# Two more blocks of an MLP by seven products of quarters, two fewer as filler for attention

## The chip, the cores and the metric

One core of a Trainium2 chip. The metric is the device time of one execution in microseconds (us); each kernel was run several times, and a profile was taken of one execution. On one core a run's state can only be told by its distance from the fastest run of the same kernel; every run used here counts as fast. Engines: PE is TensorE, PEld its weight loads, DVE VectorE, ACT ScalarE, POOL GpSimd, SP SyncE; a "q" behind a name is the engine's queue of issues and waits.

## The reference, cut to what matters

```python
# 8 batches x 8 heads, 576 rows of 64; then an MLP of 4608 tokens, 512 -> 2048 -> 512, all float32
scores = scale * q @ k.T
scores = np.where(scores >= scores.max(-1) - tau, scores, -1e9)
attn = np.exp(scores - scores.max(-1)); attn = attn / (attn.sum(-1) + 1e-9)
x = heads_side_by_side(attn @ v)            # 4608 x 512
h = x @ w_in                                # 4608 x 2048
out = (0.5 * h * (1 + erf(h / sqrt(2)))) @ w_out
```

## The kernel before

Attention goes by pairs of heads, 32 in all, each in five chunks: four of 128 rows for both heads, one with the last 64 rows of both. The MLP goes by 18 blocks of 256 tokens. Ten of them are "plain": they are dealt out between the chunks as filler, so that TensorE has work while DVE does the softmax. The last eight are done at the end in four "duos", each two blocks by seven products of quarters in place of eight (a matrix product cut into quarters takes eight smaller products, or seven and some more sums).

What matters for this study is how a pair's results come together. After the softmax of a chunk DVE transposes it in 32 by 32 squares; SyncE then issues copies that regroup the squares, for chunks 0 and 1 together, 2 and 3 together, and the short chunk. The row sums become divisors, which this kernel sends through DRAM to spread them over the partitions; in the next pair's chunk 2, P is multiplied by V, and DVE divides the product.

```python
def divisors(p):                                   # after chunk 4
    ...                                            # DVE: add, reciprocal, transpose the sums
    nc.sync.dma_start(rows..., turned)             # L401: sums to DRAM
    for e in range(2):
        nc.sync.dma_start(to[:, 0:MAIN]..., src)   # L407: divisors back, to every partition
        nc.sync.dma_start(to[:, MAIN:S]..., src)   # L409

def regroup(p, i):
    for a in range(4):
        if i == NC:                                # the short chunk: 4 "tail" copies, L432
            nc.sync.dma_start(s["pT"][e][...], pd_tail[p % 2][rows])
            continue
        for e in (1, 0):                           # 8 copies after chunk 2, 8 after chunk 3, L436
            nc.sync.dma_start(s["pT"][e][...][:, :, half], pd[e][rows, :, half])

# one chunk of pair p (cut; made[] are the two divisions of the pair before, in chunk 2 only)
scores(p, i); softmax_head(p, i)                   # PE; DVE reduce, ACT exp, DVE threshold
softmax_tail(p, i)                                 # DVE multiply by the mask, with the row sum
if made: made[0]()                                 # DVE L466, waits for the divisors
turn_p(p, i)                                       # DVE transposes
if made: made[1]()
if i == 2: regroup(p, 1)
if i > 2: regroup(p, i)
if i == NC: divisors(p)
if i == 1: load(p + 2)                             # 16 loads of q, k, v issued by GpSimd
if i == 2: turn_qk(p + 1)                          # DVE transposes of the next pair's q and k
fill(...)                                          # PE: filler from the plain blocks
```

## Time and profile before

| | before |
|---|---|
| median of its first 3 runs | 1435.5 us (1433.5 to 1439.47) |
| span of the profiled run | 1434.2 us |
| pair period in the attention, pairs 4 to 31 | (1008.6 - 179.9) / 27 = 30.7 us |
| busy TensorE in that stretch | 99% |
| four duos, 1037.3 to the end | 397 us |

The lines that carry the prediction stand in it. Three more of the same view of waits are needed for the comparison: engine and line, what it waited for, us in total, times, longest.

```profile
DVE p L379 <- ACT p L361: 25.0, 51, 1.1
...
DVE x L466 <- PE xT L448: 7.9, 3, 3.2
...
PE sc L349 <- DVE p L379: 8.5, 11, 2.9
```

The first is DVE at its masked multiply, waiting for ScalarE's exp; the second DVE at its division, waiting for the product to divide; the last is TensorE at the scores, waiting for DVE to free the banks. All are small beside DVE's own wait for TensorE's scores, 105.5 us in the prediction: mostly it is TensorE that is late.

### The profile page before, as it was taken

What the parts mean: (1) busy time and instruction counts of PE and PEld (TensorE: products, weight loads), DVE (VectorE), ACT (ScalarE), POOL (GpSimd) and SP (SyncE); (2) the same over time, 40 slices, a digit from 0 to 9 for tenths busy, and PEclk for the clock granted to TensorE, in tenths of its full rate; (3) what the DMA queues carried; (4) which work ended last, traced back from release to release, by engine and by line L of the source; (5) the groups of instructions that cost most, each with busy time, mean ns of one, the idle gap of its engine ahead of it and who ended that gap; (6) DMA issues with size and microseconds to landing.
All of it is one profiled execution on the core that took longest, in us unless ns stands there. A gap on an engine that the chain in (4) does not pass through costs nothing.

```text
span 1434.2 us, 19357 instructions
## 1 busy us (share of the span) xinstructions
PE 1389.7 (97%) x6544; PEld 962.9 (67%) x6544; DVE 941.1 (66%) x2088; ACT 640.3 (45%) x1039; POOL 288.0 (20%) x502
## 2 busy tenths in 40 slices
PE   6899899999999999999999999999999999999999
PEld 5667546566466574664756647566488888888887
DVE  5987887886777878778788778777664132241330
ACT  5758525436355264472654726547142141230320
POOL 3121323422222433223332224300000000000000
PEclk8999999999999999999999999999999999999999
DMA  9967368897777898778988788875500100100000
GB/s 281 275 243 202 113 133 151 140 161 130 125 137 122 151 150 151 145 125 142 168 146 155 154 142 152 142 143 106 107 1 1 44 1 0 59 0 8 23 1 30
DMA packets 449489, 167.04 MB, mean 116 GB/s; under 512 B 413040, under 2 KB 432048, under 8 KB 449392
## 3 DMA queue, kind: packets, MB, share of 16 engines
q1 hardware_dynamic: 423184, 108.65, 43.0%
q0 software_dynamic: 23808, 56.57, 14.8%
q8 instruction: 53, 0.87, 0.3%
q10 hardware_dynamic: 2400, 0.59, 0.2%
q14 instruction: 44, 0.36, 0.1%
HBM read 71.68 MB, written 11.47 MB: 58 GB/s over the span
## 4 chain that ended last, share of the span: by engine, by line
PE 85%; DVE 8%; ACT 3%; DMA 1%; issue 1%; SPq 0%; DVEq 0%; ACTq 0%
PE bank L629 27%; PE hT L508 18%; PE o_ps L520 17%; PE sc L349 12%; PE xT L448 10%; DVE p L379 2%; DVE nmx L360 2%; ACT p L361 1%; DVE power L185 1%; PE tr L295 1%; DMA inv<-turned 1%; DVE mant L183 0%; DVE w_in L187 0%; ACT L488 0%; ACT L495 0%
## 5 line engine op out<-in xcount | busy, mean ns | idle before, releaser
L361 ACT ACTIVATE p<-sc,nmx 128x576 f32<-128x576 f32 x288 | 202.8, 740 | 405.2 <-DVE nmx L360 404.9
L508 PE MATMUL hT<-x,w_in 128*128 128x256 f32 x1280 | 297.3, 384 | 1.8 <-DVE x L466 1.7
L520 PE MATMUL o_ps<-w_out,g 128*128 128x512 f32 x640 | 294.6, 603 | 0.0
L508 PEld LDWEIGHTS hT<-x,w_in 128*128 128x128 f32 x1280 | 238.9, 190 | 60.0 <-issue 28.4
L360 DVE TENSOR_REDUCE nmx<-sc 128x1 f32<-128x576 f32 x288 | 205.0, 749 | 106.1 <-PE sc L349 105.5
L379 DVE SCALAR_TENSOR_TENSOR p<-sc,thr,p 128x576 f32<-128x576 f32 x288 | 225.3, 816 | 36.4 <-ACT p L361 25.0
L520 PEld LDWEIGHTS o_ps<-w_out,g 128*128 128x128 f32 x640 | 116.9, 190 | 140.7 <-issue 138.9
L448 PE MATMUL xT<-pT,v 128*64 128x288 f32 (+2 forms) x1280 | 169.4, 418 | 6.0 <-issue 5.4
L349 PE MATMUL sc<-kT,qT 64*128 64x288 f32 x960 | 167.0, 435 | 5.6 <-DVE p L379 5.2
L421 DVE STREAM_TRANSPOSE pd<-p 128x576 f32<-128x576 f32 x224 | 160.7, 756 | 3.0
L219 POOL DMA_DIRECT2D q<-in_q_dram x104 | 69.6, 675 | 462.7 <-DVE q_tail L337 349.7
L349 PEld LDWEIGHTS sc<-kT,qT 64*128 64x128 f32 x960 | 94.0, 188 | 87.7 <-issue 74.0
L448 PEld LDWEIGHTS xT<-pT,v 128*64 128x64 f32 x1280 | 93.6, 140 | 77.9 <-issue 22.7
L227 POOL DMA_DIRECT2D v<-in_v_dram x208 | 109.3, 528 | 58.6 <-DMA k<-in_k_dram 32.0
L629 PE MATMUL bank<-x,w_in 128*128 128x256 f32 x384 | 93.6, 379 | 3.2 <-DVE x L643 3.2
L495 ACT ACT_TABLE_LOAD x71 | 91.1, 1283 | 1.3
L488 ACT ACT_TABLE_LOAD x71 | 91.1, 1283 | 1.3
L629 PE MATMUL bank<-unit 128*128 128x256 f32 x352 | 87.7, 379 | 0.0
L629 PEld LDWEIGHTS bank<-x,w_in 128*128 128x128 f32 x384 | 72.9, 190 | 13.9 <-issue 4.1
L629 PEld LDWEIGHTS bank<-unit 128*128 128x128 f32 x352 | 66.9, 190 | 9.1
L629 PE MATMUL bank<-w_out,unit 128*128 128x256 f32 x320 | 72.3, 379 | 0.0
L219 POOL DMA_DIRECT2D k<-in_k_dram x104 | 68.7, 667 | 0.0
(143 smaller groups left out, 1279.9 us busy)
## 6 DMA issues: line engine op xcount, KB each, us to landing
pT<-pd SPq DMA_DIRECT2D x448, 160.0 KB, 4.8
pT<-pd_tail SPq DMA_DIRECT2D x112, 80.0 KB, 2.7
q<-in_q_dram POOLq DMA_DIRECT2D x104, 72.0 KB, 4.5
k<-in_k_dram POOLq DMA_DIRECT2D x104, 72.0 KB, 5.8
out_dram<-o_sb SPq DMA_DIRECT2D x28, 256.0 KB, 3.7
inv<-turned SPq DMA_DIRECT2D x56, 128.0 KB, 3.6
v<-in_v_dram POOLq DMA_DIRECT2D x156, 40.0 KB, 5.3
raw<-in_moe_w_out_dram POOLq DMA_DIRECT2D x10, 512.0 KB, 5.0
```

The costliest lines, as they stand in the source:

```text
L219: eng.dma_start(t[e * D + f:e * D + f + Q], rows[:, :, f:f + Q])
L227: eng.dma_start(t[r:P:4, e, 0:n, :], rows[:, r * KR:r * KR + n, :])
L349: nc.tensor.matmul(sc[e][:, h, 0:HALF], lhsT=lhsT, rhs=s["kT"][rows, at:at + HALF], start=True, stop=True)
L360: nc.vector.tensor_reduce(nmx[:, e:e + 1], sc, axis=AXIS.XY, op=ALU.max, negate=True)
L361: nc.scalar.activation(w[:, e * S:(e + 1) * S].rearrange("p (h s) -> p h s", h=2), sc, AF.Exp, bias=nmx[:, e:e + 1], scale=1.0)
L379: nc.vector.scalar_tensor_tensor(row, sc[e][:, :, 0:HALF], thr[:, e:e + 1], row, op0=ALU.is_ge, op1=ALU.mult, accum_out=den[e])
L421: nc.vector.transpose(to[:, 0:NB, :], w[:, e * S:(e + 1) * S].rearrange("p (b i) -> p b i", i=Q))
L448: nc.tensor.matmul(xT[f, 0:hi - lo], lhsT=s["v"][:, e, c, :], rhs=pT[:, c, lo:hi], start=(c == 0), stop=(c == KR - 1))
L488: nc.scalar.activation(t, hT, AF.Gelu)
L508: nc.tensor.matmul(hT[:, j % 2, :], lhsT=w_in_sb[c][:, j * P:(j + 1) * P], rhs=x_blk[n][:, c, :], start=(c == 0), stop=(c == N_DM - 1))
L520: nc.tensor.matmul(o[:, 0:d_model], lhsT=g[j][:, m * P:(m + 1) * P], rhs=w_out_sb[j], start=(j == 0), stop=(j == N_DF - 1))
L629: nc.tensor.matmul(to, lhsT=l, rhs=r, start=start and k == 0, stop=k == len(pairs) - 1, skip_group_check=not start)
```

## The change

Its intent: seven products are cheaper than eight, so do ten blocks that way; the attention then has less filler and should get shorter, and DVE and the loads are relieved so that it can.

```diff
-    PLAIN = N_BLK - 8
-    AWAY = [PLAIN, PLAIN + 1, PLAIN + 2]
+    PLAIN = N_BLK - 10
+    AWAY = list(range(PLAIN, PLAIN + 5))          # inputs of these blocks wait in DRAM
...
 def softmax_head(p, i):
     for e in range(n):
         nc.vector.tensor_reduce(nmx[:, e:e + 1], sc, ...)
+        nc.gpsimd.tensor_scalar(thr[:, e:e + 1], nmx[:, e:e + 1], -1.0, tau_eff, ...)
         nc.scalar.activation(w..., sc, AF.Exp, bias=nmx[:, e:e + 1], scale=1.0)
-    nc.vector.tensor_scalar(thr[:, 0:n], nmx[:, 0:n], -1.0, tau_eff, ...)
...
         if p >= HP and i == 1 and p + 2 < NP:
-            load(p + 2)
+            loads = load_steps(p + 2)
+        if p >= HP:
+            next(loads, None)                     # q, k, v, v: four issues a chunk
...
-    GOAL += [... [1.96, 3.3, 4.64, 5.98, 7.32, 8.66, PLAIN]]
+    GOAL += [... [1.75, 2.79, 3.83, 4.87, 5.92, 6.96, PLAIN]]
```

Cut from it: in the first four pairs the addition to the row sum goes to GpSimd and the reciprocal comes after the weight conversions; the conversions are paced a little faster, end with the first batch, and use another buffer for their last pieces.

More of the change, by code (lines that the diff above doesn't have):

```diff
@@ L67 @@
     N_BLK = B * S // TOK
-    PLAIN = N_BLK - 8
-    AWAY = [PLAIN, PLAIN + 1, PLAIN + 2]
-    order = list(range(PLAIN + 3, N_BLK)) + AWAY
+    PLAIN = N_BLK - 10
+    AWAY = list(range(PLAIN, PLAIN + 5))
+    order = list(range(PLAIN + 5, N_BLK)) + AWAY
     DUOS = list(zip(order[0::2], order[1::2]))
@@ L147, in load_piece @@
         k = loaded[0] - 1
-        if k % 2 and k < len(pieces) - 4:
+        if k % 2:
             room = pd[k // 2 % 2][:, 0:NB - 2, :].bitcast(U32).rearrange("p b i -> p (b i)")
@@ L210, in load, with load_steps @@
     def load(p):
+        for _ in load_steps(p):
+            pass
+    def load_steps(p):
         b, hp = divmod(p, HP)
@@ L219, in load @@
                     eng.dma_start(t[e * D + f:e * D + f + Q], rows[:, :, f:f + Q])
+            yield
         t = s["v"] = v_sb[p % 4]
@@ L227, in load @@
                 eng.dma_start(t[r:P:4, e, 0:n, :], rows[:, r * KR:r * KR + n, :])
+            yield
     def load_early(p):
@@ L356, in softmax_head @@
         nmx = small.tile([P, 2], FP32, tag="nmx", name="nmx")
+        thr = s["thr", i] = small.tile([P, 2], FP32, tag="thr", name="thr")
         w = s["p", i] = work.tile([P, 2 * S], FP32, tag="p", name="p")
@@ L360, in softmax_head @@
             nc.vector.tensor_reduce(nmx[:, e:e + 1], sc, axis=AXIS.XY, op=ALU.max, negate=True)
+            nc.gpsimd.tensor_scalar(
+                thr[:, e:e + 1], nmx[:, e:e + 1], -1.0, tau_eff, op0=ALU.mult, op1=ALU.subtract)
             nc.scalar.activation(
                 w[:, e * S:(e + 1) * S].rearrange("p (h s) -> p h s", h=2), sc, AF.Exp, bias=nmx[:, e:e + 1], scale=1.0)
-        thr = s["thr", i] = small.tile([P, 2], FP32, tag="thr", name="thr")
-        nc.vector.tensor_scalar(thr[:, 0:n], nmx[:, 0:n], -1.0, tau_eff, op0=ALU.mult, op1=ALU.subtract)
     def softmax_tail(p, i):
@@ L380, in softmax_tail, with diagonal @@
                 row, sc[e][:, :, 0:HALF], thr[:, e:e + 1], row, op0=ALU.is_ge, op1=ALU.mult, accum_out=den[e])
-        if p >= EARLY:
-            return
-        rden = small.tile([P, 2], FP32, tag="rden", name="rden")
-        nc.vector.tensor_scalar(pair[:, 0:n], pair[:, 0:n], 1e-9, None, op0=ALU.add)
-        nc.vector.reciprocal(rden[:, 0:n], pair[:, 0:n])
+        if p < EARLY:
+            nc.gpsimd.tensor_scalar(pair[:, 0:n], pair[:, 0:n], 1e-9, None, op0=ALU.add)
+            s["sum", i] = pair[:, 0:n]
+    def diagonal(p, i):
+        s = st[p]
+        den = s.pop(("sum", i))
+        n = den.shape[1]
+        nc.vector.reciprocal(den, den)
         diag = s["diag", i] = dg.tile([P, 2, P], FP32, tag="inv", name="diag")
         for e in range(n):
-            nc.scalar.activation(diag[:, e, :], ident, AF.Copy, bias=0.0, scale=rden[:, e:e + 1])
+            nc.scalar.activation(diag[:, e, :], ident, AF.Copy, bias=0.0, scale=den[:, e:e + 1])
     def divisors(p):
@@ L757 @@
     GOAL = [(-1, 0.0), (START - 1, 0.0), (BATCH - 1, 0.55)]
-    GOAL += [(BATCH * (m + 2) + WEIGH, x) for m, x in enumerate([1.96, 3.3, 4.64, 5.98, 7.32, 8.66, PLAIN])]
+    GOAL += [(BATCH * (m + 2) + WEIGH, x) for m, x in enumerate([1.75, 2.79, 3.83, 4.87, 5.92, 6.96, PLAIN])]
     def goal(n):
@@ L771 @@
     due = []
+    loads = iter(())
     for n in range(len(slots) + WEIGH + 1):
@@ L827 @@
         if p >= HP and i == 1 and p + 2 < NP:
-            load(p + 2)
+            loads = load_steps(p + 2)
+        if p >= HP:
+            next(loads, None)
         if p >= HP - 1 and i == 2 and p + 1 < NP:
             turn_qk(p + 1)
-        convert(3000 if n < 2 * HP else 3400)
+        convert(3000 if n < 2 * HP else 3650 if n < BATCH - 1 else 1e9)
+        if early:
+            diagonal(p, i)
         if not early:
```

## The prediction

> **What bounds the kernel now.** I read the page first, then stretches of the span, then the chain of waits, then single instructions in order of time around one attention pair, with the SyncE queue beside them.
>
> ```profile
> PE 1389.7 (97%) x6544; PEld 962.9 (67%) x6544; DVE 941.1 (66%) x2088; ACT 640.3 (45%) x1039; POOL 288.0 (20%) x502
> ...
> 180.00:1008.60 828.60, 819.26 (x3781) 499.30 (x3779) 654.56 (x1412) 415.33 (x551) 238.03 (x401) 1.00 0.81 142
> 1037.30:1434.00 396.70, 388.20 (x1793) 339.81 (x1791) 125.69 (x300) 102.06 (x258) 0.00 (x0) 1.00 0.04 16
> ```
>
> Columns of the last two: stretch, length, busy PE, PEld, DVE, ACT, POOL, granted clock, DMA share, GB/s. The first stretch is the attention of pairs 4 to 31, with ten plain MLP blocks as filler for TensorE; the second is the four duos (two blocks each) by seven products. TensorE is busy for 99% of the first, so the plain reading is "take filler out and the stage shrinks by as much". But DVE is at 79% and DMA at 0.81 there, so I looked for what comes next.
>
> ```profile
> 613.96 20.39 SPq L436 DMA_DIRECT2D pT<-pd  x16
> 634.45 3.37 SPq L432 DMA_DIRECT2D pT<-pd_tail  x4
> 637.92 0.58 SPq L401 DMA_DIRECT2D turned<-turned  x1
> 639.94 0.59 SPq L407 DMA_DIRECT2D inv<-turned  x1
> ...
> 644.39 17.92 SPq L436 DMA_DIRECT2D pT<-pd  x16
> ```
>
> One pair takes 644.39 - 613.96 = 30.4 us, and SyncE is issuing for some 27 of them. The pair's transfers hang together: 16 regroup copies (L436), 4 tails, the row sums to DRAM, four loads of divisors. DVE waits for the last of these:
>
> ```profile
> 553.29 0.52 DVE L466 TENSOR_TENSOR x<-xT,inv 128x64 f32<-128x64 f32 x2 [0.96 <-DMA inv<-turned]
> 553.73 1.43 DVE L421 STREAM_TRANSPOSE pd<-p 128x576 f32<-128x576 f32 x2
> ...
> DVE nmx L360 <- PE sc L349: 105.5, 101, 7.0
> ...
> DVE x L466 <- DMA inv<-turned: 34.7, 19, 5.2
> ...
> SPq L436 <- DVE pd L421: 74.9, 25, 44.7
> ```
>
> This is a ring. Divisors land, DVE divides, transposes chunk 2, turns the next q and k, does chunk 3 (reduce, threshold, multiply, transpose); then SyncE issues the second eight L436, the tails, the sums and the divisors, which land. Read instruction by instruction over all 27 rounds: landing to the start of the second eight is 8.0 to 10 us mostly, median 9.0; from there to the next landing 19.7 to 22.5, median 20.9, but 18.3 to 19.2 in the last rounds, which have no loads of q, k and v. Sum 29.9 against a period of 30.7 on average (27 periods from 179.9 to 1008.6). So TensorE and this ring are nearly balanced now; the ring has about 1 us of slack.
>
> **What the Trainium skill says.** "Perfetto Trace Analysis", What "DMA-bound" means: one of its forms is an issuing engine's track solid with DMA slices. SyncE at some 27 of 30.4 us agrees. "DMA: Bandwidth & Descriptors", Issuing engines are not separate DMA queues: all run on the same 16 DMA engines and interleave. Here too: with the loads absent (948 to 1009 us) the DMA share falls from 0.81 to 0.60 and the ring's SyncE half by 2 us. "GPSIMD Engine Reference", 4.1 Engine selection, prefers VectorE for elementwise work; for one element per partition this should not matter, but the trace has no such GpSimd operation (nearest: its 128x1 memset, 93 ns). "SBUF — State Buffer", SBUF: two separate sides: GpSimd and VectorE can lock each other out of a shared port pair; nothing in this trace shows it.
>
> **The change part by part.**
> 1. Two plain blocks leave the attention. A block has 128 instructions of 256 columns (20 take 4.32 us in the duos, 0.216 each: 27.6) and 64 of 512 (10 take 4.32 to 4.49: 28.2), so 55.3 to 56; two are -111 us of TensorE.
> 2. A fifth duo comes in. The chain of waits gives the others back to back, 1088.86, 1186.33, 1283.81, 1381.28: 97.5 us each. TensorE is its limit (DVE 126 of 397), and all of it is on the path: +97.5. TensorE alone would net -13, that is 0.9%.
> 3. Filler for a pair falls from 1.34/4 to 1.04/4 of a block: 4.15 us less, so TensorE needs 30.4 - 4.15 = 26.3 us for a pair.
> 4. The threshold leaves DVE: 138 x 238 ns = 32.8 us over 28 pairs, with gaps some 0.33 us a chunk. DVE was 654.6/27.1 = 24.1 us a pair, now 23.0; with the exp it waits for in the short fifth chunk and small waits for scores about 25.3. In the ring only chunk 3's threshold lies: 9.0 - 0.35, and a further 0.7 because TensorE no longer comes late with scores; I take 7.8 (shortest seen with the threshold 8.0 to 8.2). On GpSimd it lies beside the exp (740 ns), so it costs nothing unless GpSimd is issuing.
> 5. The loads: 16 issues at 0.53 to 0.68 us, 9.6 us a pair, now four at a time (2.1 to 2.7 us) behind a chunk's thresholds. The next threshold is due some 4.6 us later, so it fits. q and k go out with chunks 1 and 2, and leave the second eight's window: L436 there 9.8 us, 7.3 without loads, now about 8.2. But they then meet the sums and divisors, which I let grow by about 1. Half ring 20.9 - 1.6 + 1 = 20.2.
> 6. Two more blocks to DRAM and back: four transfers of 512 KB at 5 us, hidden; about 1 us of SyncE each.
> 7. First 180 us: thresholds, additions and part of the division's waiting leave DVE (20 x 0.4 us), conversions end earlier; DVE is over 90% busy in much of it, so about -6.
>
> Ring: 7.8 + 20.2 = 28.0 us for a pair, above TensorE's 26.3 and DVE's 25.3; the last pairs without loads nearer 26.5, so 27.7 on average. Sum: start 179.9 - 6 = 174; 27 x 27.7 = 748; rest of the last pair 26 (was 28.7); duos 396.9 + 97.5 = 494.4. Together 1442. I put 1441.
>
> **The rivals.**
> A, TensorE stays the limit: 27 x 26.5 = 716, total about 1410. For it: 99% busy now, DVE kept down on purpose, and a tuned kernel's next step is likely to have been kept for a gain. Against: the ring's 29.9, of which the change shortens only parts.
> B, as worked out: the ring of divisors, DVE and SyncE is the new bound; about four fifths of the stage's gain of 111 goes, 1441. For it: DVE waits for the divisors in most rounds already.
> C, DMA fills up: the same descriptors in less time. 0.81 x 30.7 = 24.9 us of DMA a pair in 27.7 is 0.90, and the divisors queue behind q and k, a ring of 29 or more: 27 x 29 = 783, total about 1477. Thresholds stuck behind GpSimd's issues would look alike in time, but show as DVE waiting for POOL.
> D, the divisors land faster because loads are spread better than I think: ring 27.0, total about 1423.
>
> **Range and chances.** B with D and A on one side and a mild C on the other: 1418 to 1466. Faster by over 2% means below 1407, which even A hardly reaches: 0.03. Slower by over 2%, above 1464, needs a ring of 28.6 or so: 0.12. Within 2%: 0.85.
>
> **What would show it.** Right: the duos take 5 x 97.5 = 487 us back to back; in the attention TensorE falls to about 94% busy; DVE's wait for inv appears in nearly every pair and grows to some 2 to 4 us; the second eight L436 start about 8 us after that landing; pair period 27 to 28.5; the DMA share near 0.88; the wait of DVE for scores falls well below 105 us. Wrong: a period near 26.3 with TensorE at 99% (A), divisors landing 12 us or more after the tails (C), DVE waiting for POOL's thresholds, or a duo that is not 97.5 us.

## The result, and the profile after

| | before | after |
|---|---|---|
| median | 1435.0 us (4 runs) | 1468.89 us (4 runs, 1466.58 to 1476.4) |
| ratio | | 1.0238 (1.0201 to 1.0275) |
| span of the profiled run | 1434.2 us | 1474.3 us |
| pair period | 30.7 us | (948.5 - 177.5) / 27 = 28.6 us |
| busy TensorE in that stretch | 99% | 732 of 771 us, 95% |
| after the attention, from the first matmul of the duos | 397 us | 498 us |

Ratios here and below are the mean time of a kernel's fast runs over that of the fast runs of before in the same rounds, so they are not quite the ratios of the medians beside them. The ratio of the changed kernel takes in a fifth run (1469.03 us). Its profiled run, 1476.4 us, is about 7 us slower than the median.

First the stretches of the changed kernel; columns as in the prediction.

```profile
177.50:948.50 771.00, 731.64 (x3415) 430.97 (x3414) 620.01 (x1277) 383.80 (x510) 320.92 (x661) 0.99 0.77 153
980.00:1474.00 494.00, 486.77 (x2236) 426.16 (x2236) 150.90 (x361) 125.88 (x320) 0.00 (x0) 0.99 0.05 17
```

The attention stage lost 58 us (829 to 771) and the duos gained 101. TensorE is no longer full, and neither is any other engine: DVE 80%, DMA 0.77. So I looked for a chain. The view of waits of the changed kernel shows where:

```profile
DVE x L478 <- DMA inv<-turned: 72.3, 23, 8.0
...
DVE p L386 <- ACT p L370: 61.4, 155, 1.2
...
PE sc L355 <- DVE p L386: 36.6, 39, 3.0
...
DVE nmx L367 <- PE sc L355: 31.2, 32, 7.0
```

The wait for the divisors has doubled (34.7 before). TensorE now waits for DVE (8.5 to 36.6), and DVE seldom for TensorE (105.5 to 31.2). The second line is worth a look: DVE waits 36 us more for the exp, which is nearly all of the 37.9 us that the thresholds took on it. They left DVE, but less than half of that could be used, as DVE then waits for the exp of the same chunk: from the start of the reduce to that of the first multiply a chunk took 1.79 us before and 1.64 after (medians of 160 chunks), 0.15 of the 0.33 us that the prediction counts for a threshold.

One round of the ring, from the order of time around one pair: first SyncE's queue, then the two divisions that stand at its ends.

```profile
576.58 15.71 SPq L448 DMA_DIRECT2D pT<-pd  x16
592.39 3.18 SPq L444 DMA_DIRECT2D pT<-pd_tail  x4
595.68 0.59 SPq L413 DMA_DIRECT2D turned<-turned  x1
597.68 0.59 SPq L419 DMA_DIRECT2D inv<-turned  x1
...
604.34 2.46 SPq L448 DMA_DIRECT2D pT<-pd  x3
```
```profile
575.93 0.52 DVE L478 TENSOR_TENSOR x<-xT,inv 128x256 f32<-128x256 f32 x2 [1.18 <-DMA inv<-turned]
...
603.49 0.52 DVE L478 TENSOR_TENSOR x<-xT,inv 128x256 f32<-128x256 f32 x2 [0.99 <-DMA inv<-turned]
```

DVE divides the moment the divisors land, at 575.9, and again at 603.5: 27.6 us, with a wait at both ends. TensorE stands in that circle only with the scores of chunk 3, for which DVE waited 0.7 us in this round.

And the duos, from the chain that ended last:

```profile
1031.26 96.97 PE bank L641 x448
1128.74 96.97 PE bank L641 x448
1226.21 96.97 PE bank L641 x448
1323.69 96.97 PE bank L641 x448
```

97.5 us each, as before.

### The profile page after: what moved, and what is told of

It reads as the page before. It is cut to its first block, busy times and chain, and to the rows that moved or that the text cites. A ratio compares the mean times of both kernels' runs of the same rounds, so it can differ in the third digit from the quotient of the medians.

```text
span 1474.3 us, 20023 instructions
## 1 busy us (share of the span) xinstructions
PE 1390.7 (94%) x6608; PEld 977.5 (66%) x6608; DVE 923.9 (63%) x1974; ACT 634.6 (43%) x1062; POOL 388.9 (26%) x810
## 4 chain that ended last, share of the span: by engine, by line
PE 61%; DVE 17%; ACT 8%; DMA 8%; issue 3%; POOL 2%; SPq 1%; DVEq 0%; POOLq 0%; ACTq 0%
PE bank L641 33%; PE sc L355 8%; PE o_ps L532 8%; PE hT L520 7%; DVE p L386 4%; DVE nmx L367 4%; ACT p L370 4%; PE xT L460 4%; DMA k<-in_k_dram 3%; DVE pd L433 3%; POOL k L223 1%; ACT L500 1%; ACT L507 1%; DMA turned<-turned 1%; PE tr L301 1%
## 5 line engine op out<-in xcount | busy, mean ns | idle before, releaser
L520 PE MATMUL hT<-x,w_in 128*128 128x256 f32 x1024 | 244.1, 389 | 0.0
L532 PE MATMUL o_ps<-w_out,g 128*128 128x512 f32 x512 | 238.9, 604 | 0.0
L520 PEld LDWEIGHTS hT<-x,w_in 128*128 128x128 f32 x1024 | 192.6, 193 | 52.0 <-issue 25.8
L367 DVE TENSOR_REDUCE nmx<-sc 128x1 f32<-128x576 f32 x288 | 204.1, 745 | 35.2 <-PE sc L355 31.2
L368 POOL TENSOR_SCALAR thr<-nmx,tau_eff 128x1 f32<-128x1 f32 x288 | 85.0, 295 | 493.0 <-DVE nmx L367 492.7
L532 PEld LDWEIGHTS o_ps<-w_out,g 128*128 128x128 f32 x512 | 92.3, 189 | 110.2 <-issue 108.4
L641 PE MATMUL bank<-x,w_in 128*128 128x256 f32 x480 | 117.8, 381 | 4.4 <-DVE x L655 4.4
L641 PE MATMUL bank<-unit 128*128 128x256 f32 x440 | 110.5, 381 | 0.0
L641 PEld LDWEIGHTS bank<-x,w_in 128*128 128x128 f32 x480 | 91.8, 191 | 17.8 <-issue 5.2
L641 PE MATMUL bank<-w_out,unit 128*128 128x256 f32 x400 | 90.4, 379 | 0.0
L641 PEld LDWEIGHTS bank<-w_out,unit 128*128 128x128 f32 x400 | 76.0, 190 | 10.3
```

The lines of the kernel that those rows point to most:

```text
L367: nc.vector.tensor_reduce(nmx[:, e:e + 1], sc, axis=AXIS.XY, op=ALU.max, negate=True)
L520: nc.tensor.matmul(hT[:, j % 2, :], lhsT=w_in_sb[c][:, j * P:(j + 1) * P], rhs=x_blk[n][:, c, :], start=(c == 0), stop=(c == N_DM - 1))
L532: nc.tensor.matmul(o[:, 0:d_model], lhsT=g[j][:, m * P:(m + 1) * P], rhs=w_out_sb[j], start=(j == 0), stop=(j == N_DF - 1))
L641: nc.tensor.matmul(to, lhsT=l, rhs=r, start=start and k == 0, stop=k == len(pairs) - 1, skip_group_check=not start)
```

## The experiments

Theory: with ten blocks the ring (divisors land, DVE's chunk 3, SyncE's second eight copies, tails, sums, divisors) sets the pair's period. Rivals: DMA is simply full; DVE's work is the limit; thresholds or loads on GpSimd cost the time themselves. In the table "period" is the time from the first regroup copies of pair 4 to those of pair 31, over 27, and "wait" DVE's wait for the divisors in the whole run.

| run | median us | ratio | period us | wait us |
|---|---|---|---|---|
| after | 1468.9 | 1.0238 | 28.6 | 72 |
| after, again | 1471.2 | 1.0239 | 28.8 | 77 |
| ten blocks alone | 1487.4 | 1.0342 | 29.1 | 89 |
| the rest alone, eight blocks | 1429.9 | 0.9941 | 30.7 | 10 |
| no wait for the divisors | 1438.7 | 1.0006 | 27.5 | gone |
| tails from ScalarE | 1582.7 | 1.1001 | 32.6 | 5 |
| late divisions | 1447.4 | 1.0055 | 27.7 | 26 |
| thresholds on DVE | 1481.2 | 1.0293 | 29.0 | 89 |
| loads in one go | 1565.9 | 1.0877 | 32.0 | 8 |
| two more copies of the sums | 1490.5 | 1.0355 | 29.2 | 91 |
| the same with eight blocks | 1430.0 | 0.9951 | 30.5 | 22 |
| late divisions with eight blocks | 1429.1 | 0.9943 | 30.5 | 6 |

Differences in us between runs of different rounds are taken from the ratios, 0.001 being 1.44 us. All results were correct but that of "no wait".

**Ten blocks alone**: the kernel before with the first and the last piece of the diff above.

> The kernel before with ten blocks by seven products, five kept in DRAM and the new filler schedule, and nothing else of the change. Ring theory: the divisor ring stays as before, about 29.5 us a pair (chunk 3 of DVE 8.5, SyncE half 20.9), 0.9 us over the changed kernel's 28.6, so about 1490 us. Rival 'the moved thresholds or split loads cost the time': without them the kernel is faster than the changed one, 1440 us or less. Rival 'the other parts do nothing': 1469 us, as the changed one.

Measured 1487.4 us. The ring theory's time holds; the period is 29.1 us and not 29.5 (read as below, DVE's half of the ring is 8.3 and SyncE's 20.5, for 8.5 and 20.9). The other parts, thresholds, loads and the first pairs' order, are worth 0.0342 - 0.0238, 15 us together, and are no part of the loss.

**The rest alone**: the changed kernel with eight blocks.

```diff
-    PLAIN = N_BLK - 10
+    PLAIN = N_BLK - 8        # and AWAY, order and GOAL as before
```

> The changed kernel with eight blocks, three kept in DRAM and the old filler schedule: thresholds on GpSimd, loads in four portions and the reordered divisions alone. Ring theory: TensorE needs 30.4 us a pair and the ring only 28.3, so TensorE alone sets the period, 30.4 in place of 30.7, and the time is about 1425 to 1430 us, slightly faster than before. Rival 'thresholds on GpSimd cost time by themselves': 1445 us or more.

Measured 1429.9 us, as expected in size, but not for the stated reason: the period stayed at 30.7. The gain is ahead of it: the first regroup copies of pair 4 stand at 173.3 us, before at 179.9. This version is 0.6% faster than the kernel before (0.9921 to 0.9962, small but clear of the noise), so it beats both kernels; the two variants of it further down do not differ from it.

**No wait for the divisors**: DVE multiplies by resident data; the same transfers and operations remain (result wrong on purpose).

```diff
-   nc.vector.tensor_tensor(to, x, by[:, at:at + size], op=ALU.mult)
+   nc.vector.tensor_tensor(to, x, w_in_sb[0][:, at:at + size], op=ALU.mult)
```

> The changed kernel, but DVE multiplies by a resident constant in place of the loaded divisors, which are still loaded as before (result wrong on purpose). Only the wait is gone. Ring theory: the period falls from 28.6 us to the next limit, TensorE's 26.3 or the regroup copies' own loop of about 26.8, so 45 us less, about 1425 us. Rival 'DMA is simply full' or 'DVE's work is the limit': the same transfers and the same DVE work remain, so 1465 us, no change.

Measured 1438.7 us, ratio 1.0006 against 1.0238: 33 us for one wait. DMA moves the same bytes in less time and DVE does the same work, so neither was the limit. The gain stopped 14 us short of what I expected. Its stretch of attention:

```profile
172.90:914.90 742.00, 725.99 (x3415) 429.86 (x3413) 621.67 (x1276) 383.33 (x510) 320.07 (x661) 1.00 0.81 159
```

TensorE is busy for 726 of 742 us, 98%, and DVE's wait for scores is back up from 31 to 60 us. I read from this that the next limit is TensorE itself, at 26.9 us a pair and not the 26.3 that I had worked out, with 0.6 us of waits between chunks; no run tests that. So even without this wait ten blocks only draw level with the kernel before.

**Tails from ScalarE**: to take four issues out of SyncE's part of the ring.

```diff
-   nc.sync.dma_start(s["pT"][e][:, :, MAIN + at:...], pd_tail[p % 2][rows])
+   nc.scalar.dma_start(s["pT"][e][:, :, MAIN + at:...], pd_tail[p % 2][rows])
```

> The changed kernel with the four tail copies of a pair issued from ScalarE's queue, so the sums and divisors stand 3.4 us earlier in SyncE's queue; result correct. Ring theory: ring 28.3 - 3.4 = 24.9, so the period falls to about 27 (TensorE 26.3, regroup loop, ScalarE held for 2.5 us a pair by the issues), about 1430 us. Rival 'DMA full': no change, 1465 us. Rival 'ScalarE's exp becomes the limit': 1465 us or more.

Measured 1582.7 us, a clear miss. The wait for the divisors did go (72 to 5 us), but in its place came others. In the order of time, three of ScalarE's four issues, the exp behind them and the multiply that needs it:

```profile
618.88 0.95 ACTq L444 DMA_DIRECT2D pT<-pd_tail  x1
...
619.95 2.36 ACTq L444 DMA_DIRECT2D pT<-pd_tail  x2
622.35 1.37 ACT L370 ACTIVATE p<-sc,nmx 128x576 f32<-128x576 f32 x2 [2.48 <-issue]
...
623.20 0.82 DVE L386 SCALAR_TENSOR_TENSOR p<-sc,thr,p 128x576 f32<-128x576 f32 x1 [3.15 <-ACT p L370]
```

ScalarE issues the four copies in order with its exps, from 618.2 to 622.3, and 18 times it also waited for earlier copies to land (view of waits: 67 us for pT<-pd, 36 for pT<-pd_tail). DVE's wait for the exp rose from 61 to 152 us. The third rival of that run was right: the cure put its wait on a busier engine. It does not speak against the ring, whose wait it removed; it shows that issues are not free where the issuer has timely work.

**Late divisions**: the two divisions go behind chunk 2's transposes and the turning of q and k, so that only they and chunk 3 lie between landing and second eight.

```diff
-        if made: made[0]()
         turn_p(p, i)
-        if made: made[1]()
 ...
             turn_qk(p + 1)
+        for divide in made:
+            divide()
```

> The changed kernel, with the two divisions of a pair moved behind chunk 2's transposes and the next pair's turning of q and k; result correct, same work on every engine and queue. Ring theory: of the 7.75 us between the divisors' landing and the second eight regroup copies only the two divisions (1.0) and chunk 3 (4.6) are left, so the ring is 28.3 - 2.1 = 26.2 us, below what the run without the wait left (27.3), and the time is about 1440 us. Rival 'DVE's or DMA's work as such is the limit': 1469 us.

Measured 1447.4 us, ratio 1.0055: 26 us less than the changed kernel for an order of instructions, with all work kept. I had expected about 1440. The wait for the divisors and the stretch of attention, columns as before:

```profile
DVE x L478 <- DMA inv<-turned: 26.3, 12, 6.7
...
177.30:925.50 748.20, 726.32 (x3415) 429.80 (x3413) 622.84 (x1275) 383.36 (x510) 319.55 (x661) 1.00 0.80 158
```

The period is 27.7, close to what no wait at all gives, with TensorE at 97%. This and the run without the wait are the two that carry the verdict.

**Thresholds on DVE**, with loads still in four portions.

> The changed kernel with the thresholds back on DVE, one operation for both columns as before; loads still in four portions. Ring theory: only chunk 3's threshold lies in the ring, and DVE had to wait for the exp anyway in its place (the wait for exp was 25 us before and 61 after), so it costs 0.2 to 0.35 us a pair, 5 to 9 us, about 1476 us. If the thresholds were worth their whole 0.33 us in every chunk, 0.33 x 5 x 27 = 45 us, 1513 us. Rival 'GpSimd's thresholds hold DVE up': faster, 1460 us or less.

Measured 1481.2 us, 8 us more by the ratios (1.0273 to 1.0314 against 1.0201 to 1.0275, which just touch): the move of the thresholds is worth about what lies in the ring, and far from the 45 us that they would cost in every chunk.

**Loads in one go**, thresholds on GpSimd.

> The changed kernel with a pair's sixteen loads issued in one go, thresholds still on GpSimd. GpSimd then issues for 9.6 us behind chunk 1, and chunk 2's thresholds come behind them: some 5 us late once a pair. But chunk 2 lies ahead of DVE's wait for the divisors, which has a slack of about 1 to 3 us: so I expect about 3 us a pair more, 1550 us, with DVE waiting for POOL. If the order of loads does not matter: 1469 us.

Measured 1565.9 us, 92 us more, 16 beyond the estimate. The view of waits and one chunk in the order of time:

```profile
DVE p L386 <- POOL thr L368: 175.4, 28, 9.3
```
```profile
600.60 0.57 POOL L368 TENSOR_SCALAR thr<-nmx,tau_eff 128x1 f32<-128x1 f32 x2
600.95 0.82 DVE L386 SCALAR_TENSOR_TENSOR p<-sc,thr,p 128x576 f32<-128x576 f32 x1 [9.31 <-POOL thr L368]
```

Once a pair the thresholds stand behind GpSimd's issues, 6.3 us on average (175.4 / 28). The portions are needed once the thresholds are on GpSimd: they hold this loss off. What they are worth by themselves no run shows: thresholds on DVE with loads in portions is 7 us below ten blocks alone, but has the first pairs' new order too, and its pair 4 starts 4.7 us earlier (174.4 for 179.1).

**Two more copies of the sums** in SyncE's queue, to spare DRAM; then the same with eight blocks.

```diff
+        for _ in range(2):
+            nc.sync.dma_start(spare..., turned)
         nc.sync.dma_start(rows..., turned)
```

> The changed kernel with two more copies of the sums to spare DRAM issued by SyncE ahead of the real one, 0.58 us each: 1.16 us of SyncE a pair, inside the ring, and next to nothing for DMA (16 KB each). Ring theory: 27 x 1.16 = 31 us more, about 1500 us. Rival 'the limit is TensorE, DVE or the bytes that DMA moves': 1469 to 1473 us.

> Eight blocks with all the rest of the change (1430 us, 30.4 us a pair) and the two spare copies of the sums in SyncE's queue. With ten blocks they cost 17 us. Ring theory: with eight blocks the ring has slack under TensorE, so they cost at most 3 us: ratio to the kernel before 0.994 to 0.997. If extra issues of SyncE cost the same wherever they stand: 17 us more, ratio 1.006.

Measured: ratio 1.0355 with ten blocks, 17 us more than the changed kernel; 0.9951 with eight, 1.4 us more than the rest alone, with intervals that overlap. SyncE's added time counts only where the ring sets the period. It was half of the 31 us expected. Averaged over the rounds, the real copy starts 1.15 us later in the queue, but lands 2.40 us after its start instead of 2.76 (perhaps because the copies ahead of it have had longer to drain; not tested); the ring as a whole went from 28.27 to 28.91 us.

**Late divisions with eight blocks**, and **the changed kernel again** beside them.

> Eight blocks with all the rest of the change, and the divisions moved late. With ten blocks the move was worth some 25 us. Ring theory: with eight blocks TensorE sets the period, so the move is worth nothing: ratio within 0.003 of 0.994. Were the divisions' place worth something by itself: 0.98 or less.

> The changed kernel unaltered, on the same chip and in the same rounds as the two others, so that the differences between experiments can be read against it: ratio 1.024 as before, its period 28.3 to 28.7 us and the divisor wait on DVE in most pairs.

Measured 0.9943 and 1.0239, the latter with a period of 28.8 us, a little over the 28.7 expected, and the divisor wait 22 times. The move that is worth 26 us with ten blocks is worth nothing with eight.

## Why the prediction was right or wrong

The time is outside the range: 1469 us against 1441 and at most 1466. The mechanism B, the ring in place of TensorE, was right. The step that failed is the size of its period: 27.7 us was put into the sum, and 28.6 was measured, 23 of the 32 us by which the profiled run missed.

- *The duos, +97.5 us.* Each is 97.5 us. The stage from its first matmul to the end grew by 101.5 (396.9 to 498.4), as its start got slower: DVE's sums of x came later (a wait of 4.4 us for 3.2), and the twelve matmul instructions after that wait took some 1.9 us for four, where the later ones take 1.03. In the repeat the stage took 495.5 us, so most of that excess is not steady.
- *DVE's half of the ring, 7.8 us.* Measured, instruction by instruction over 27 rounds: 7.75.
- *SyncE's half, 20.2 us.* Measured 20.5. The second eight fell by 1.85 us where I took 1.6; sums and divisors grew by 1.6 where I took 1 (the landing of the sums 2.1 to 2.76, that of the last divisors after its issue 3.18 to 4.12). So SyncE's half gained nothing from the split loads, what the second eight saved coming back as later landings: ten blocks alone, with the loads as before, has 20.5 too.
- *The ring, 28.0 us, and then "27.7 on average".* Here the prediction failed. The ring's mean is 28.3 and the period 28.56, and 27 x (28.56 - 27.7) is 23 us. About a third of it is SyncE's half, 20.5 for 20.2. Another third is the 0.3 us that I took off because the last pairs have no loads: those do fall, to 26.6 to 27.9 us in the last three, but others are longer and I gave them nothing. The last third is that the period is counted from pair 4's first copies, ahead of the first round, and the first period took 32.9 us. Among the longer rounds are the three in which inputs of blocks go to DRAM, transfers that I had called hidden: 30.5, 30.5 and 32.8 us, against a mean of 28.0 for the others before the last three, 10 us in all. In the seven traces with ten blocks other than tails from ScalarE and loads in one go, these three rounds lie 1.9 to 3.6 us above the others; but other rounds at the same place in their batch of four pairs, without such a trip, also reach 31.6. That the trips cause it is read from their place and was not tested.
- *The sum.* Start 177.5 for 174 (172.7 in the repeat), 27 periods 771 for 748, rest of the last pair and duos 525.8 for 520.4: 3.5 + 23 + 5.4 is the 32 us by which the profiled run missed; the median missed by 28. In the repeat the 27 periods alone account for 29 us (776.5).
- *First 180 us, -6.* Between 2 and 7 us in the changed kernel's two profiles and the rest alone.
- *Thresholds, 0.33 us a chunk.* The ring's share was right (8 us for moving it back); outside the ring DVE waits for the exp in their place.
- *SyncE issuing for 27 of 30.4 us, and 1 us of slack.* The pair that the prediction shows is an unusual one, with 26.2 us of issues; over all 27 pairs they take 23.7 of 30.7 us, so SyncE's queue was not near full. The slack compares a sum of medians, 29.9, with a mean period; the mean of the same rounds is 30.5, as a few are long (34.7, 34.6, 33.0). Neither changed the forecast.
- *The DMA share near 0.88.* It came out at 0.77, 22.0 us a pair where the prediction carried 24.9 over unchanged. Why these transfers kept the DMA engines busy for less time stays open.
- *TensorE at 26.3 us a pair.* Not the bound, so unseen in the time; without the wait it proved to be 26.9. Against before, the filler's matmuls took 103 us less in the 27 periods of that run, where 4.15 a pair makes 112, and those of scores and products 10 us more.
- *Rivals.* A, TensorE staying the limit, is out: 95% busy, and 33 us less without the wait. C, divisors landing late, was true in part, 1.6 us instead of 1; as a statement that DMA is full it is refuted by the run without the wait, which had a DMA share of 0.81 against 0.77. Thresholds stuck behind GpSimd's issues come only with loads in one go (DVE waits 175 us for them there, 2.2 in the changed kernel). D, shorter landings, is out.
- *Chances.* Slower by over 2% had 0.12 and was the outcome. That was too little: by the prediction's own count a period of 28.6 us was enough for it, 0.6 us above its estimate of the ring, and the rounds of the kernel before already spread over several us.

What stays open: why the matmuls of scores and products take longer with ten blocks, and how much of the longer rounds is due to the blocks' trips to DRAM.

## What to carry to other kernels

When an engine is full, look for the ring that is nearly as long before taking work off it: a wait that appears in most rounds, however short, is a reason to measure the ring (before the change it came 19 times, with TensorE still the limit), and less work on the engine then pays only down to the ring's length. Measure such a ring end to end and over all rounds, and put the mean of all of them, with the bad ones, into the sum; then shorten it by order first, moving the operation that waits behind those that need not. The same step (late divisions, two more issues) gains or costs 17 to 26 us where the ring binds and next to nothing where it has slack, so test it in both.

## What the Trainium skill lacked or had wrong

- "DMA: Bandwidth & Descriptors", Issuing engines are not separate DMA queues, says that initiating a DMA is usually small relative to the DMA itself. Here SyncE's issue of a 160 KB copy within SBUF took 0.61 us at the least and 0.97 in the median of before, against 4.8 from issue to landing, a fifth, but they add up: 23.7 of 30.7 us a pair, and 26.2 in the pair that the prediction shows. From ScalarE, four copies stood among its work from 618.2 to 622.3 us, and ScalarE stood idle for 2.5 us before the exp behind them.
- "GPSIMD Engine Reference", 4.1 Engine selection, has no figure for a small operation with a scalar operand: 128x1 took 295 ns on GpSimd, where 128x2 took 237 on VectorE. Nor does it say that operations stand in order behind the engine's own DMA issues: with a pair's sixteen loads issued in one go, VectorE waited up to 9.3 us for a threshold.
- "Perfetto Trace Analysis", Identifying the Most-Contended Engine, goes by the engine of highest occupancy (TensorE rather by its weight loads and rate of work, DMA by its use of HBM). In the changed kernel's attention DVE had 80% and the weight loads 56%, and removing DVE's wait of 72 us brought 33 us with DVE's work kept. Its section on dependency chains says how to follow a wait, but not that a ring across pairs sets a period of its own.
